# A two-layer transformer on one Trainium2 core: layer two's first query unit takes its last tile of keys as a segment of its own

## The chip, the core and the metric

The kernel runs on one core of one Trainium2 chip. The metric is the device time of one execution in microseconds, as the median of several runs. The profile is that of one further execution, taken by the hardware profiler.

The engines are TensorE (PE in the profile, PEld its weight loads), VectorE (DVE), ScalarE (ACT), GpSimd (POOL) and SyncE (SP), which issues most DMAs; POOL issues some. Each engine takes its instructions in the order written. Matmul results go to PSUM, of which the kernel uses eight banks: one for the running sum of value products, seven in one shared pool.

## The reference

Two layers, each an attention with one key and value head for 16 query heads of 28 elements, and a gated feed-forward part; x has 2048 rows of 448.

```python
def _A_ref(x, wq, wk, wv, wo):
    q = (x @ wq).reshape(B, S, H, Dh).transpose(0, 2, 1, 3)
    k = x @ wk
    v = x @ wv
    scores = einsum("bhqd,bkd->bhqk", q, k) * (Dh ** -0.5)
    o = einsum("bhqk,bkd->bhqd", softmax(scores), v)
    return o.transpose(0, 2, 1, 3).reshape(B, S, H * Dh) @ wo
def _B_ref(x, w_gate, w_up, w_down):
    return (sigmoid(x @ w_gate) * (x @ w_up)) @ w_down
for _ in range(2):
    x = x + _A_ref(_layernorm(x), A_wq, A_wk, A_wv, A_wo)
    x = x + _B_ref(_layernorm(x), B_w_gate, B_w_up, B_w_down)
```

The softmax subtracts each row's maximum over all 2048 keys.

## The kernel before, in words

**Units and steps.** A unit u is 128 queries with all 16 heads, so a layer (l = 0 or 1 in the code) has 16 units. Keys come in 16 tiles of 128, kt. The main loop (line 1081) runs 256 steps a layer, 16 for each unit. A step makes four score products (line 584, 512 columns each, four heads at a time), four exps on ScalarE into a tile P (line 587), and, one or two steps later, value products (pv, line 595: eight matmuls for a step) that add into the one bank for value sums. After a unit's last key tile ScalarE copies the sum to pvs (line 599).

**Order by hand.** PATHS gives the order inside an even and an odd step: S a score with its exp, P the value products of one waiting step, M a place for maxima, X a tick of the side chains, F a slice of filler. For layer two's first three units it is path C, "FFSXSSSPPM" in even and "SFFXFFSMSSF" in odd steps.

**Filler.** Everything on TensorE that isn't attention (query projections, gate, up and down products) comes from generators that fill.slice runs a few matmuls at a time, first in, first out. In layer two's first steps only query projections of later blocks are in it; the first feed-forward block (bulk) is added when units 0 and 1 have been normed.

**Maxima.** The row maxima are found before the scores, from rough products (mx, line 549): a group is four matmuls over up to 512 keys into four banks of the shared pool, and four reductions on VectorE (line 554). A unit has 16 groups; unit 0 of layer two has finer ones at the end, group 14 for keys 1792 to 1920 and group 15 for the last 128. When all groups of a unit are done, row_max (line 565) reduces them to a row m; a few places later fin turns m on TensorE (mt, line 575), copies it to mr (line 577), and POOL issues a DMA (line 578) that writes it as row 28 of the query tile QS, from where the score product itself subtracts it. Scores of a unit may thus start only when the row has landed. In layer two's first 48 steps a group is done at M only in the steps listed in sparse (line 1071): i * 47 // n for i below n, where n is the number of groups of units 0 to 3 still open, plus four. Else M only visits the list late, whose entries are the fins that wait.

**The seam of the layers.** When layer one's steps are over, a tail loop (line 1131) runs the last feed-forward block, and between its slices groups of maxima for layer two's units 0 to 3, as far as keys are there. For each finished tile of 128 rows a chain of stages follows: norm (db), turn (dct), keys and values (dd), turn of the keys (det), and df, which counts the tile as done (KVD). The list fine gets an entry when the last tile's output is there and another after its turn; from the first on, slices come after the stages. Group 14 of unit 0 may go only when fine holds two entries. The loop ends when all chains are empty and all groups of unit 0 are done. A further slice of filler follows (line 1151, QCH, the cost of eleven query products), then the waiting fins run (line 1062), another half slice (line 1078), and the steps of layer two begin.

**Query projection of block 1.** Its four groups of eleven products (qp) are filler at the seam. ScalarE copies each result twice, POOL subtracts (line 414) and issues the store to DRAM (qd, line 421).

**Buffers.** h has HB buffers, the scratch tag s2 three, pvs one, P twelve; at the start the first HB row tiles of x lie in h's buffers, the others in P's.

## Time and profile before

| what | value |
|---|---|
| time, median of 3 runs | 2247.47 us (2243.81 to 2251.59) |
| the profiled execution | 2247.71 us, span 2245.9 us |
| TensorE busy | 2195.5 us (98%) |
| VectorE busy | 1643.7 us (73%) |
| ScalarE busy | 1552.8 us (69%) |
| GpSimd busy | 335.9 us (15%) |
| exps (line 587) | 2048 of 690 ns in the mean |
| reductions of maxima (line 554) | 2048 of 682 ns in the mean |

The span runs from the first to the last instruction; the time holds a little more. A row of a timeline has the start and the length in us, the engine, the line, the operation, what is written from what, the shapes and how many instructions were merged (x4); in square brackets stands how long the engine had been idle before it and what ended that. Matmuls are pipelined and their ends are modelled, so starts are the safer reading. A time such as 1222.88 counts from the start of the span. The seam of the layers lies near 1220 us.

### The profile page before, as it was taken

The numbers are of one execution on the slowest core, as the hardware profiler recorded it, in microseconds if no ns is written. First come the engines' busy times: TensorE is split into PE (matmuls) and PEld (weight loads), VectorE is DVE, ScalarE is ACT, GpSimd is POOL, SyncE is SP. The second block draws the span as 40 slices with busy tenths as digits, with TensorE's granted clock in tenths as the row PEclk, the third lists the DMA queues.
The fourth block names the chain that finished last, engine by engine and source line by source line (L and its number), as shares of the span: only waits on it lengthen the run. The fifth ranks groups of instructions, "written<-read, shape, count | busy, mean of one in ns | idle before, by whom it ended". The sixth has DMA issues, their size and how long they took to land.

```text
span 2245.9 us, 41454 instructions
## 1 busy us (share of the span) xinstructions
PE 2195.5 (98%) x15915; PEld 1030.8 (46%) x15915; DVE 1643.7 (73%) x2905; ACT 1552.8 (69%) x2595; POOL 335.9 (15%) x590
## 2 busy tenths in 40 slices
PE   7998999999999999999999999999999999999999
PEld 3322344444544445454564324445454544445467
DVE  7888888777777787777796557777777777777222
ACT  5698777776667677676614997777676767777741
POOL 5113764101010100101012010000000000000010
PEclk9999999999999999999999999999999999999999
DMA  4333662323313232331441113323231313223233
GB/s 143 106 97 94 197 215 81 106 79 85 112 60 102 64 100 90 97 107 49 119 154 35 36 52 108 80 88 99 67 108 49 100 59 103 76 88 96 75 118 108
DMA packets 203622, 213.28 MB, mean 95 GB/s; under 512 B 135376, under 2 KB 164240, under 8 KB 203424
## 3 DMA queue, kind: packets, MB, share of 16 engines
q1 hardware_dynamic: 198080, 195.78, 29.2%
q0 software_dynamic: 5344, 14.87, 1.9%
q8 instruction: 124, 2.03, 0.4%
q14 instruction: 74, 0.61, 0.1%
HBM read 175.37 MB, written 23.59 MB: 89 GB/s over the span
## 4 chain that ended last, share of the span: by engine, by line
PE 86%; DVE 8%; ACT 2%; issue 1%; DMA 1%; SPq 1%; POOL 0%; DVEq 0%; ACTq 0%; POOLq 0%
PE pv L595 20%; PE s L584 19%; PE up L352 11%; PE dn L784 11%; PE gp L352 11%; PE mx L549 7%; DVE mp L554 6%; PE wo L695 3%; PE qp L352 2%; ACT P L587 1%; DMA wgu<-wgu_d 0%; DMA rq<-in_A_wq_dram 0%; DMA rc<-sums 0%; PE hot L916 0%; DVE sgu L131 0%
## 5 line engine op out<-in xcount | busy, mean ns | idle before, releaser
L587 ACT ACTIVATE P<-s,esc 128x512 f32<-128x512 f32 x2048 | 1297.8, 690 | 474.5 <-PE s L584 462.8
L554 DVE TENSOR_REDUCE mp<-mx 128x1 f32<-128x512 f32 x2048 | 1269.4, 682 | 389.2 <-PE mx L549 385.4
L584 PE MATMUL s<-QS,KK 96*128 96x512 f16 x2048 | 673.8, 381 | 21.3 <-DVE mp L554 14.8
L352 PEld LDWEIGHTS <-wgu 128*128 128x128 f16 x4928 | 467.6, 97 | 182.1 <-issue 42.9
L595 PE MATMUL pv<-P,VV 128*32 128x512 f32 x4096 | 510.7, 602 | 0.0
L352 PE MATMUL gp<-XT,wgu 128*128 128x256 f16 x2464 | 349.2, 272 | 2.4 <-DVE mp L554 1.7
L352 PE MATMUL up<-XT,wgu 128*128 128x256 f16 x2464 | 348.3, 272 | 0.7 <-DVE mp L554 0.7
L784 PE MATMUL dn<-WD,h 128*128 128x448 f16 x1344 | 301.0, 352 | 0.0
L584 PEld LDWEIGHTS <-KK 96*128 96x128 f16 x2048 | 189.7, 97 | 212.5 <-issue 114.5
L595 PEld LDWEIGHTS pv<-P,VV 128*32 128x32 f32 x4096 | 98.7, 108 | 244.6 <-issue 242.6
L549 PE MATMUL mx<-KK,QH 32*128 32x512 f16 x1792 | 185.3, 386 | 3.0 <-DVE mp L554 1.7
L784 PEld LDWEIGHTS <-h 128*128 128x128 f16 x1344 | 126.5, 97 | 129.4 <-issue 14.5
L549 PEld LDWEIGHTS <-QH 32*128 32x128 f16 x1792 | 46.0, 91 | 256.5 <-issue 252.7
L669 POOL TENSOR_TENSOR lb<-pvs,lb 128x512 f32<-128x512 f32 x32 | 41.1, 1284 | 739.1 <-DMA lb<-sums 619.8
L757 ACT ACTIVATE h<-th 128x512 f16<-128x512 f32 x112 | 70.3, 628 | 61.8 <-DVE th L754 61.5
L754 DVE SCALAR_TENSOR_TENSOR th<-th,up 128x512 f32<-128x512 f32 x112 | 76.2, 680 | 48.9 <-PE up L352 42.2
L306 POOL TENSOR_SCALAR rs<-mv 128x1 f32<-128x1 f32 (+1 forms) x50 | 11.2, 225 | 656.6 <-DVE mv L291 573.6
L352 PE MATMUL qp<-XT,WQ 128*128 128x512 f16 x352 | 108.3, 390 | 0.7 <-DVE mp L554 0.4
L746 ACT ACTIVATE th<-gp,gsc 128x512 f32<-128x512 f32 x112 | 76.8, 685 | 32.8 <-PE gp L352 32.6
L758 DVE SCALAR_TENSOR_TENSOR h<-th,h 128x512 f16<-128x512 f32 x112 | 79.9, 713 | 20.8 <-ACT h L757 20.8
L695 PE MATMUL wo<-WO,oT 128*128 128x448 f16 x384 | 89.7, 352 | 0.2 <-ACT P L587 0.2
L352 PEld LDWEIGHTS <-WQ 128*128 128x128 f16 x352 | 32.9, 99 | 54.9 <-issue 28.9
(151 smaller groups left out, 918.1 us busy)
## 6 DMA issues: line engine op xcount, KB each, us to landing
wgu<-wgu_d SPq DMA_DIRECT2D x224, 512.0 KB
QS<-qd SPq DMA_DIRECT2D x384, 32.0 KB
lb<-sums SPq DMA_DIRECT2D x128, 64.0 KB
xr<-in_A_x_dram SPq DMA_DIRECT2D x32, 224.0 KB
qd<-qst POOLq DMA_DIRECT2D x28, 256.0 KB, 2.7
wgu_d<-sgu POOLq DMA_DIRECT2D x14, 512.0 KB, 3.7
x2d<-x SPq DMA_DIRECT2D x16, 224.0 KB
xr<-x2d SPq DMA_DIRECT2D x16, 224.0 KB
```

Source lines behind the costliest of these rows:

```text
L352: nc.tensor.matmul(ps, a, b, start=n == 0, stop=n == 10)
L549: nc.tensor.matmul(ps[h][:, i * w:(i + 1) * w], qh[32 * h:32 * h + 32, g], KK[l][32 * h:32 * h + 32, 1, ka:kz], start=True, stop=True, til ...
L554: nc.vector.tensor_reduce(o, ps[h].rearrange("p (g k) -> p g k", g=n), axis=AX.X, op=OP.max)
L584: nc.tensor.matmul(s, KK[l][0:96, 0, kt * 128:(kt + 1) * 128], QS[l, u][:, g].rearrange("p h n -> p (h n)"), start=True, stop=True)
L587: nc.scalar.activation(p, s, AF.Exp, scale=esc)
L595: nc.tensor.matmul(v[32 * g:32 * g + 32], VV[l][:, kt], P[g], start=kt == 0, stop=kt == KT - 1, tile_position=(0, 32 * g))
L695: nc.tensor.matmul(p, v["oT"][:, a, h * 128:(h + 1) * 128], WO[:, c, h], start=n == 0, stop=n == 11)
L746: defer(lambda: nc.scalar.activation(th, gp.rearrange("p j n -> p (j n)"), AF.Tanh, scale=gsc))
L754: nc.vector.scalar_tensor_tensor(t, th, 1.0, up.rearrange("p j n -> p (j n)"), op0=OP.add, op1=OP.mult)
L757: nc.scalar.activation(h[:, 0], t, AF.Copy, scale=2.0 ** -17)
L758: defer(lambda: nc.vector.scalar_tensor_tensor(h[:, 1], t, 2.0 ** -17, h[:, 0], op0=OP.mult, op1=OP.subtract), 3)
L784: nc.tensor.matmul(p, hs[f // 2][:, a, o:o + 128], WD[:, f, c], start=n == 0, stop=n == 3 * FC - 1)
```

## The change

Unit 0 of layer two (halved) is split into two segments: key tiles 0 to 14, and tile 15 (CUT). The first fifteen steps use a row of maxima over 1920 keys; when they are through, a second row over all 2048 keys is written into the same place of QS, and step 15 uses it. Value sums of the two segments are separate: the first is copied to pva, multiplied by exp(old row - new row), which is spread over the partitions by way of DRAM (fd, fb), and added to the second on POOL.

The tail loop ends when fine is not empty and all groups of unit 0 but group 15 are done; stages of tile 15 that are left then run at the ticks of layer two's first steps, and df follows two ticks after det instead of five. At M of the first 48 steps the first group whose keys are there is taken; groups of units 0 and 1 are done in every step, others in the steps of sparse. The fin of unit 1 waits for one visit instead of four. A fin of the second segment waits until the scores of the first have been issued. HB goes from 10 to 8, s2 from 3 to 2 buffers, pvs from 1 to 2. Tables (STEPS, FETCH, ENDS) replace the arithmetic on step numbers.

```diff
-    TB, WB, HB = 2, 4, 10
+    TB, WB, HB = 2, 4, 8
...
-                f = wk1.tile([128, 512], F32, tag="s2", name="qf", bufs=3)
+                f = wk1.tile([128, 512], F32, tag="s2", name="qf", bufs=2)
...
+    QS, QH, PVS, PVA, ROW = {}, {}, {}, {}, {}
+    fd = [drm.tile([16, 128], F32, name=f"fd{i}") for i in range(2)]
+    fsc = cst.tile([128, 1], F32, name="fsc")
+    CUT = 15
+    scaled, SCB = set(), {}
+
+    def rescale(l, u):
+        if (l, u) in SCB and (l, u) in PVA:
+            nc.gpsimd.tensor_tensor(PVA[l, u], PVA[l, u], SCB.pop((l, u)), op=OP.mult)
+            scaled.add((l, u))
+
+    def halved(l, u):
+        return l == 1 and u == 0
+
+    def segments(l):
+        out = []
+        for u in range(U):
+            out += [(u, 0, CUT), (u, CUT, KT)] if halved(l, u) else [(u, 0, KT)]
+        return out
...
-        ends = [0, 512, 1024, 1536] + ([1792, 1920] if l and u == 0 else []) + [2048]
+        ends = [0, 512, 1024, 1536] + ([1792, 1920] if l and (u == 0 or halved(l, u)) else []) + [2048]
...
-            self.left = {u: len(groups_of(l, u)) for u in range(U)}
+            self.left = {}
+            for a in todo:
+                p = a[0], self.part(a)
+                self.left[p] = self.left.get(p, 0) + 1
...
+        def part(self, a):
+            return int(halved(self.l, a[0]) and groups_of(self.l, a[0])[a[1]][1] >= CUT * 128)
...
-            return not any(a[0] == 0 for a in self.todo)
+            return not any(a[0] == 0 and not (halved(self.l, 0) and self.part(a)) for a in self.todo)
...
-                if late[i][0] <= 0 and late[i][2] in QS:
+                if late[i][0] <= 0 and late[i][2] in QS and (not late[i][3] or ("s",) + late[i][2] in stored):
...
-            self.left[u] -= 1
-            if not self.left[u]:
-                row_max(l, u, self.mp.pop(u), todo[-1][0] + 1)
+            p = self.part((u, j))
+            self.left[u, p] -= 1
+            if not self.left[u, p]:
+                whole = p or not halved(l, u)
+                row_max(l, u, mp, todo[-1][0] + 1 if whole else kb + 1, p)
+                if whole:
+                    self.mp.pop(u)
...
-    def row_max(l, u, mp, n):
+    def row_max(l, u, mp, n, part):
...
-            stored.add(("m", l, u))
+            stored.add(("m", l, u, part))
             p = fps([16, 128], F16, "mt")
             nc.tensor.transpose(p, m16, id16)
-            r = wk1.tile([16, 128], F16, name="mr")
+            if halved(l, u) and not part:
+                r = ROW[l, u] = wk1.tile([16, 128], F16, name="mra", bufs=1)
+            else:
+                r = wk1.tile([16, 128], F16, name="mr")
             nc.vector.tensor_copy(r, p)
             (nc.gpsimd if l or u else nc.sync).dma_start(QS[l, u][28:29].rearrange("o g h n -> o (g h) n"), r)
-        late.append([4 if l and u in AHEAD else LT, fin, (l, u)])
-
-    def scores(l, u, kt, g, P):
-        assert ("m", l, u) in stored, (l, u, kt)
+            if part:
+                f = wk1.tile([16, 128], F32, tag="s2", name="fe", bufs=2)
+                nc.vector.tensor_tensor(f, r, ROW.pop((l, u)), op=OP.subtract)
+                nc.scalar.activation(f, f, AF.Exp, scale=fsc[0:16])
+                nc.sync.dma_start(fd[u % 2], f)
+                v = {}
+
+                def spread():
+                    v["b"] = wk1.tile([128, 512], F32, tag="lb", name="fb", bufs=1)
+                    for g in range(G):
+                        nc.sync.dma_start(v["b"][32 * g:32 * g + 32], fd[u % 2].rearrange("(g h) n -> g (h n)", g=G)[g:g + 1]
+                                          .to_broadcast([32, 512]))
+                    return
+                    yield
+
+                def scale():
+                    SCB[l, u] = v["b"]
+                    rescale(l, u)
+                    return
+                    yield
+                later((1, spread), (1, scale))
+        late.append([4 if l and u in AHEAD[1:] else LT, fin, (l, u), part])
+
+    def scores(l, u, kt, a, z, g, P):
+        assert ("m", l, u, int(a > 0)) in stored, (l, u, kt)
...
+        if kt == z - 1 and g == G - 1:
+            stored.add(("s", l, u))
+
+    def pv(l, u, kt, a, z, P):
+        if kt == a:
             PVS[l, u] = psv.tile([128, 512], F32, tag="v", name="pv")
         v = PVS[l, u]
         for g in range(4):
-            nc.tensor.matmul(v[32 * g:32 * g + 32], VV[l][:, kt], P[g], start=kt == 0, stop=kt == KT - 1,
+            nc.tensor.matmul(v[32 * g:32 * g + 32], VV[l][:, kt], P[g], start=kt == a, stop=kt == z - 1,
                              tile_position=(0, 32 * g))
-        if kt == KT - 1:
-            o = wk1.tile([128, 512], F32, name="pvs", bufs=1)
+        if kt == z - 1 and z < KT:
+            o = PVA[l, u] = wk1.tile([128, 512], F32, name="pva", bufs=1)
             nc.scalar.copy(o, v)
+            rescale(l, u)
+        elif kt == z - 1:
+            o = wk1.tile([128, 512], F32, name="pvs", bufs=2)
+            nc.scalar.copy(o, v)
+            if a:
+                assert (l, u) in scaled
+                nc.gpsimd.tensor_tensor(o, o, PVA.pop((l, u)), op=OP.add)
             PVS[l, u] = o
...
-                th = wk1.tile([128, 512], F32, tag="s2", name="th", bufs=3)
+                th = wk1.tile([128, 512], F32, tag="s2", name="th", bufs=2)
...
-                    later((2, db), (1, dct), (1, dd), (1, det), (5, df))
+                    later((2, db), (1, dct), (1, dd), (1, det), (2, df))
...
-        junk = wk1.tile([128, D], F32, tag="s2", name="junq", bufs=3)
+        junk = wk1.tile([128, D], F32, tag="s2", name="junq", bufs=2)
...
+        nc.vector.tensor_scalar(fsc, esc, 32768.0, None, op0=OP.mult)
...
+    STEPS, FETCH, ENDS = {}, {}, {}
+    for l in range(layers):
+        seg = segments(l)
+        STEPS[l] = [(u, kt, a, z) for u, a, z in seg for kt in range(a, z)]
+        end = {u: i for i, (u, *_) in enumerate(STEPS[l])}
+        begin = {u: min(i for i, t in enumerate(STEPS[l]) if t[0] == u) for u in range(U)}
+        FETCH[l] = {begin[u - 1] + 2: u for u in range(1, U)}
+        ENDS[l] = {i + 2: u for u, i in end.items()}
...
-            u, kt = divmod(step, KT)
+            u, kt, lo, hi = STEPS[l][step]
...
-            for o in pair[kt % 2]:
+            for o in pair[step % 2]:
                 if o == "S":
-                    scores(l, u, kt, len(P), P)
+                    scores(l, u, kt, lo, hi, len(P), P)
                 elif o == "M":
+                    a = next((a for a in mx.todo if not l or KVD[l] * 128 >= mx.need(a)), None)
                     if l and step < 3 * KT:
-                        n = step in sparse
+                        n = int(step in sparse or a[0] < 2) if a else 0
                     else:
                         n = 1 + (u == 0 and kt in MORE)
                     if not n:
                         mx.visit()
                     for _ in range(n):
-                        if not mx.step() and not final and l + 1 in mxs:
+                        if not mx.step(a if l else None) and not final and l + 1 in mxs:
                             a = mxs[l + 1].between()
                             if a and soon(a[0], mxs[l + 1].need(a)):
                                 mxs[l + 1].step(a)
-                    if kt == 2 and u + 1 < U:
-                        load_qs(l, u + 1)
+                    if step in FETCH[l]:
+                        load_qs(l, FETCH[l][step])
...
-                    if u and kt == 1:
-                        b = (u - 1) // TB
-                        if (l, b) not in BLK:
-                            BLK[l, b] = Block(l, b)
-                        later(*BLK[l, b].tile(u - 1))
+                    if step in ENDS[l]:
+                        w = ENDS[l][step]
+                        if (l, w // TB) not in BLK:
+                            BLK[l, w // TB] = Block(l, w // TB)
+                        later(*BLK[l, w // TB].tile(w))
...
-            waiting.append((l, u, kt, P))
+            waiting.append((l, u, kt, lo, hi, P))
...
-        while side or pend or (fill.gens if final else not nx.started()):
+        while (side or pend or fill.gens) if final else not (fine and nx.started()):
```

3 lines of the change are left out of this document (removed).

## The prediction

> **What bounds the kernel now.** I read the page first, then a table of windows over the run, then the engines' timelines around the layers' seam, and last the steps behind it.
>
> ```profile
> span 2245.9 us, 41454 instructions
> PE 2195.5 (98%) x15915; PEld 1030.8 (46%) x15915; DVE 1643.7 (73%) x2905; ACT 1552.8 (69%) x2595; POOL 335.9 (15%) x590
> ```
>
> ```profile
> 1200.00:1220.00 20.00, 16.61 (x143) 8.15 (x141) 14.81 (x31) 8.26 (x18) 7.94 (x10) 0.99 0.24 72
> 1220.00:1240.00 20.00, 19.10 (x105) 6.07 (x105) 8.45 (x15) 16.60 (x29) 1.75 (x3) 0.92 0.08 27
> 1225.00:1345.00 120.00, 115.62 (x718) 36.53 (x718) 67.36 (x119) 112.51 (x191) 12.94 (x25) 1.00 0.14 41
> 1500.00:1600.00 100.00, 99.81 (x739) 47.98 (x732) 78.30 (x134) 70.62 (x115) 9.01 (x20) 1.00 0.24 72
> ```
>
> The windows' columns are the stretch, its length, busy time of PE, weight loads, DVE, ACT and POOL, granted clock, DMA share and rate. TensorE is full nearly everywhere (99.81 of 100 us at 1500). Two places are not. At the seam, 1200 to 1220, it is idle for 3.39 us. From 1225 to 1345, layer two's first three units, nothing of its feed-forward work is ready; there TensorE (115.62 of 120) and ScalarE (112.51) are both nearly full. What delays that stretch delays the end, because the full stretch behind it cannot catch up. Here is the seam on TensorE:
>
> ```profile
> 1212.46 0.34 PE L335 MATMUL t<-id,hl 128*128 128x128 f16 x3 [0.24 <-DVE hl L323]
> 1212.73 0.40 PE L549 MATMUL mx<-KK,QHB 32*128 32x128 f16 x16
> 1213.07 1.47 PE L352 MATMUL qp<-XT,WQ 128*128 128x512 f16 x6
> 1214.37 0.45 PE L352 MATMUL kv<-WKV,XT 128*128 128x56 f16 x11
> 1214.66 1.46 PE L352 MATMUL qp<-XT,WQ 128*128 128x512 f16 x6
> ...
> 1216.07 0.38 PE L352 MATMUL qp<-XT,WQ 128*128 128x512 f16 x1
> 1216.69 0.41 PE L549 MATMUL mx<-KK,QHB 32*128 32x128 f16 x16 [0.24 <-ACT KK L392]
> 1220.14 0.28 PE L575 MATMUL mt<-id,m 128*16 128x128 f16 x1 [3.05 <-DVE m L570]
> 1220.35 2.74 PE L352 MATMUL qp<-XT,WQ 128*128 128x512 f16 x6
> 1222.88 1.10 PE L584 MATMUL s<-QS,KK 96*128 96x512 f16 x4
> ```
>
> Tile 15 is turned (t), group 14 of unit 0's maxima runs, then its keys (kv), then group 15 (1216.69); 3.05 us pass until the row of maxima is turned (mt), 2.74 more until the first score. The six products at 1220.35 need 2.53 us instead of 1.3 (six by 0.22, as in the row at 1214.66): after the idle time the clock is halved, as the 0.92 of that window says. So 3.05 + 0.24 + 0.24 + 1.2, or 4.7 us, is the most that the seam can give.
>
> **The seam after the change.** By the code the tail's loop ends one turn after tile 15's transposes, since group 14 may go only then (fine must hold two entries). Norm and turn thus stay ahead of the steps; keys and group 15 move behind. Left between group 14 and the scores are the 13 query products (6, 6 and 1 above), the row's turn and its DMA.
>
> ```profile
> 1213.16 2.49 DVE L554 TENSOR_REDUCE mp<-mx 128x4 f32<-128x512 f32 x4 [0.76 <-PE mx L549]
> ...
> 1219.62 0.25 DVE L569 TENSOR_REDUCE m<-mp 128x16 f32<-128x96 f32 x1
> ```
>
> ```profile
> 1217.52 0.73 POOL L421 DMA_DIRECT2D qd<-qst  x1 [1.41 <-DMA qd<-qst]
> 1218.27 1.16 POOL L414 TENSOR_TENSOR qst<-qf,qst 128x512 f16<-128x512 f32 x1
> 1219.74 0.73 POOL L421 DMA_DIRECT2D qd<-qst  x1 [0.31 <-POOL qst L414]
> 1220.97 0.53 POOL L578 DMA_DIRECT2D QS<-mr  x1 [0.49 <-DVE mr L577]
> ```
>
> The first fence is DVE's timeline, the second POOL's. Group 14 is reduced by 1215.65 (1213.16 + 2.49). From the row's own maximum (1219.62) to mt (1220.14) it took 0.52, so mt could run at 1216.2, and the scores 2.74 later, at 1218.9: 4.0 us earlier. But the row's DMA is issued by POOL, and the loop is followed by a slice of filler that ends the query projection of block 1: its fourth group (subtraction at 1218.27, store at 1219.74) is then queued on POOL ahead of the row. Both are where the third store, which waited until 1217.52 for an earlier transfer, put them; nothing in the change moves that. POOL is free at 1220.47 instead of the 1220.97 at which it issued the row before. So the first score comes **0.5 us** earlier, between 0 and 4.0.
>
> What moves behind the first score costs there: keys 0.29 us of TensorE (1214.37 to 1214.66), three small copies on ScalarE, group 15 0.4. Beside two nearly full engines I take **+0.4**, from 0 (all hidden) to 0.9.
>
> **The steps: one pair of them, then two with more maxima.** A pair of steps holds eight scores, eight exps, value products of two steps, and before one group of maxima.
>
> ```profile
> 1255.69 0.40 PE L549 MATMUL mx<-KK,QHB 32*128 32x512 f16 x4
> 1256.11 2.48 DVE L554 TENSOR_REDUCE mp<-mx 128x1 f32<-128x512 f32 x4 [2.64 <-PE mx L549]
> 1256.44 4.81 ACT L587 ACTIVATE P<-s,esc 128x512 f32<-128x512 f32 x8 [0.20 <-PE s L584]
> 1257.45 0.38 PE L584 MATMUL s<-QS,KK 96*128 96x512 f16 x1 [0.18 <-DVE mp L554]
> 1259.06 1.93 PE L595 MATMUL pv<-P,VV 128*32 128x512 f32 x16
> 1260.92 0.40 PE L549 MATMUL mx<-KK,QHB 32*128 32x512 f16 x4
> ```
>
> ```profile
> L549 PE MATMUL mx<-KK,QHB x76: 371/385/385, 1223.9 to 1319.9; 32*128 32x512 f16 x76
> ```
>
> ```profile
> 98.30:124.20 25.90, 10.74 (x32) 3.11 (x32) 1.00 0.11 39
> 1232.00:1284.40 52.40, 24.82 (x81) 7.73 (x81) 1.00 0.12 34
> ...
> 98.30:124.20 25.90, 3.15 (x32) 0.80 (x32) 1.00 0.11 39
> 1232.00:1284.40 52.40, 4.07 (x40) 1.01 (x40) 1.00 0.12 34
> ```
>
> The pair lasts 5.23 us (1255.69 to 1260.92). A group holds four of the seven banks that scores share; the score at 1257.45 waits for the second reduction. The last four rows are windows of the scores (first two) and of the maxima (last two). In layer one's early stage, 25.90 us hold 32 scores and 32 maxima matmuls, two groups a pair: 6.48 us a pair. In layer two 52.40 us hold 80 scores and 40 maxima matmuls, one group a pair: 5.24. A second group costs 1.24.
>
> The 76 matmuls are 19 groups of units 1 to 3 left at layer two's start. The old list of chosen steps has 19 + 4 = 23 entries, all even: 0, 2, 4. The new one has 24, and i*47//24 gives 0 and then odd steps: 1, 3, 5. Beside it the new rule forces a group in every step once the keys are there (step 3): group 15, then unit 1's four, steps 3 to 7. So groups run in 0, 1, 3, 4, 5, 6, 7 and then every odd step: 26 instead of 23. Three pairs (0-1, 4-5, 6-7) get a second one; two at 1.24, the first, which has no value products yet, at half: 3.1. Later, where TensorE is full, two groups fewer remain (one of unit 0 is added): -0.8, at 0.40 a group. Net **+2.3**, from 0.4 (only TensorE's 0.40 for each of the three, less 0.8) to 3.7 (three at 1.24, nothing back).
>
> From step 8 on the group stands inside the odd step instead of at the even one's end, in about 20 pairs. No row of layer two shows that order. At best it frees the wait ahead of the score at 1257.45 (0.18 a pair, -3.6). At worst the scores ahead of the value products wait for one more of the four reductions (2.48/4 = 0.6 us) in every third pair, while a query product holds a bank of its own: 0.2 a pair, +4. I take **+1**, near the middle, for want of a nearer row.
>
> **The cut at step 15.** The second row of maxima overwrites the first in the query tile, so it may go only when step 14's scores are out; the code lets it go at step 14's last place, and step 15 begins with a score. TensorE works in order, so everything behind that score waits: filler, value products, the group.
>
> ```profile
> 1250.41 0.22 PE L575 MATMUL mt<-id,m 128*16 128x128 f16 x1
> ...
> 1250.67 0.21 DVE L577 COPY mr<-mt 16x128 f16<-16x128 f16 x1 [1.03 <-PE mt L575]
> ...
> 1251.18 0.52 POOL L578 DMA_DIRECT2D QS<-mr  x1 [0.51 <-DVE mr L577]
> ...
> 1263.48 3.00 ACT L587 ACTIVATE P<-s,esc 128x512 f32<-128x512 f32 x5
> ...
> 1264.18 1.92 PE L595 MATMUL pv<-P,VV 128*32 128x512 f32 x16
> ...
> 1266.33 0.63 ACT L599 COPY pvs<-pv 128x512 f32<-128x512 f32 x1
> ```
>
> At the seam mt to score took 2.74 us; unit 1's row took nearly the same from mt to its issue, 0.77 (1250.41 to 1251.18) against 0.83. With 0.28 for mt itself TensorE stands 2.5 us, and ScalarE runs dry meanwhile. **+2.4**, from 1.2 (exps still queued cover half) to 3.0.
>
> The value products of step 14 and of step 15 now go to different sums, but there is one bank for them. In the row at 1264.18 both run as one block of sixteen; the copy at 1266.33 came when five exps ahead of it on ScalarE were through. After the change step 14's eight end at 1265.1 of that clock, the copy still waits for the exps until 1266.33 and ends at 1266.96, and step 15's eight, due at 1265.1, stand behind it: **+1.9**, from 0.6 (the copy alone) to 2.5. Rescaling and adding lie on POOL, which was idle there, and only the unit's row sums wait for them: nothing.
>
> **Clock.** 3.05 us of idling cost 1.2 us at half rate. After the change TensorE has its query products done by about 1217.5 and stands until 1222.4, and again 2.5 us at step 15; in each place some of the slow work lies beside ScalarE's. Half a microsecond each: **+1.0**, from 0 to 2.4. The Trainium skill (TensorE: Matmul & The Clock Gate, Part 1) says that the clock falls after about one idle window of 3.4 us; by it the first wait would count and the second not, and the sum would be 0.5 lower. The row at 1220.35 disagrees: 3.05 us were enough.
>
> **Edits at nothing.** Two h buffers and one scratch buffer fewer: seven h live in a block and value products of the block ahead are through before the next block's first h; the next block's gate and up products hide the exchange, and without that cover a block's first h would come late by about a copy (0.63 at 1266.33). Fetch and end tables give the same steps as before for whole units.
>
> **Sum.** -0.5 + 0.4 + 2.3 + 1.0 + 2.4 + 1.9 + 1.0 = +8.5 us; all ends together reach from -5.4 to +16.5. The profiled execution took 2247.7 us (1.8 of it outside the span) and becomes 2256.2; the median of the runs, 2247.5, lies 0.2 below: 2256.0. About 0.3% (6.7 us) is what a measurement can tell from no change.
>
> **Rivals.** *POOL is not in the way*: the scores start at 1218.9, 3.5 more is won, sum +5.0: 2252.5. For it: the store's place depends on one slice; against it: seven products remain and the slice has room for eleven. 0.15. *The steps absorb the added groups*: with the groups in odd steps a pair falls to ScalarE's 4.81, which is 0.43 less in 20 pairs, -8.6 in place of +1.0: 2246.4, not slower. It decides if the reductions always end before the fourth score behind them; the 6.48 us pairs speak against it. 0.15. *Both, and the cut half hidden by queued exps*: 3.5 and 1.2 less again, 2241.7, at the edge of faster. 0.1. *The odd steps drag*: +4 in place of +1, and the clock's upper end, 1.4 more: 2260.4. 0.1. That the change does only half of what it says, since the turn stays ahead of the steps, is in the forecast.
>
> My forecast has 0.5. The range, 2243 to 2264, takes in the first two rivals, the fourth, and the upper ends. Slower by over 0.3%, above 2254.2: three quarters of the forecast, the fourth rival and a third of the first, 0.52. Faster by as much, below 2240.7: most of the third rival, 0.09. Within: 0.39.
>
> **What would show it.** After: the row's DMA on POOL right behind a store (near 1220.5); first score 1222.4; groups in steps 3 to 7 with pairs over 6 us; a gap of 2.5 us ahead of step 15's first score, put down to the QS DMA; one near 2 us ahead of pv at step 16, put down to ScalarE. I am wrong if the first score comes near 1219, or if 48 steps last no longer than before.

## The result, and the profile after

| | before | after |
|---|---|---|
| time, median of 3 runs | 2247.47 us (2243.81 to 2251.59) | 2268.36 us (2267.41 to 2269.84) |
| profiled execution | 2247.71 us, span 2245.9 | 2268.36 us, span 2266.6 |

After by before is 1.0102, with a 95% interval of 1.0088 to 1.0115 (the two medians alone give 1.0093): slower by about 21 us, where 8.5 were predicted and 2264 was the upper end. The page of the kernel after, in the lines that were shown of before (span, busy time of the engines):

```profile
span 2266.6 us, 41491 instructions
PE 2206.3 (97%) x15916; PEld 1029.9 (45%) x15916; DVE 1643.1 (72%) x2910; ACT 1557.4 (69%) x2597; POOL 341.2 (15%) x593
```

TensorE has one matmul more, and is busy 10.8 us longer: matmuls that run at half clock last longer (the score at 1227.94 below takes 0.63 us, the one at 1222.40, which starts at full clock, 0.39), and matmuls that start further apart overlap less. The other 10 us are idle time. To see where both lie, both traces are cut at the same pieces of work: the first score of layer two's step 0, then of steps 2, 8, 14, 16, 18, 48, and 64 to the last. (The time of layer one differs by some us between any two profiles, even of kernels that are equal up to there, so everything is counted from layer two's first score.) Kernel before, a table of windows (stretch, its length, busy time and count of PE, weight loads, DVE, ACT, POOL, then granted clock, DMA share, rate):

```profile
1222.88:1226.79 3.91, 3.50 (x17) 1.31 (x15) 2.45 (x4) 3.41 (x6) 0.00 (x0) 0.98 0.00 0
1226.79:1242.27 15.48, 14.96 (x96) 4.63 (x95) 7.48 (x13) 15.13 (x27) 0.75 (x1) 1.00 0.05 18
1242.27:1258.10 15.83, 15.41 (x97) 4.79 (x96) 8.96 (x18) 15.05 (x26) 1.25 (x2) 1.00 0.05 18
1258.10:1263.12 5.02, 4.84 (x33) 1.51 (x32) 2.28 (x4) 4.60 (x9) 0.00 (x0) 1.00 0.00 0
1263.12:1268.45 5.33, 5.09 (x32) 1.50 (x31) 2.69 (x6) 5.33 (x11) 0.00 (x0) 1.00 0.01 2
1268.45:1350.46 82.01, 79.20 (x491) 25.22 (x490) 45.99 (x82) 75.70 (x129) 12.12 (x24) 1.00 0.20 56
...
1412.05:2155.81 743.76, 743.18 (x5465) 358.42 (x5462) 529.66 (x903) 538.60 (x871) 54.73 (x119) 1.00 0.27 83
```

The same steps of the kernel after:

```profile
1222.40:1230.31 7.91, 6.36 (x31) 1.83 (x32) 3.74 (x7) 5.20 (x11) 0.00 (x0) 0.52 0.00 0
1230.31:1252.07 21.76, 20.38 (x115) 5.52 (x114) 13.11 (x24) 15.53 (x27) 0.75 (x1) 0.86 0.04 13
1252.07:1269.12 17.05, 16.06 (x97) 4.62 (x96) 8.71 (x17) 15.03 (x26) 1.27 (x2) 1.00 0.05 17
1269.12:1276.71 7.59, 5.26 (x34) 1.51 (x33) 2.82 (x7) 5.16 (x10) 0.52 (x1) 1.00 0.08 22
1276.71:1283.97 7.26, 5.87 (x34) 1.46 (x33) 2.91 (x6) 6.07 (x12) 2.54 (x2) 1.00 0.06 15
1283.97:1371.20 87.23, 82.34 (x493) 24.81 (x491) 46.39 (x83) 76.11 (x128) 12.24 (x24) 1.00 0.19 52
...
1432.79:2175.59 742.80, 742.30 (x5457) 358.12 (x5454) 523.50 (x895) 539.69 (x871) 55.36 (x119) 1.00 0.28 83
```

Row by row, the second column of one minus that of the other gives the account of the change. Steps 0 and 1 lose 4.0 us (7.91 against 3.91, at a clock of 0.52). Steps 2 to 7 lose 6.3, the six behind them 1.2, the pair with the cut 2.6, the pair behind it 1.9, steps 18 to 47 lose 5.2, and the long full stretch gives 1.0 back. With the first score 0.5 earlier the sum is 19.7 of the 20.7 us by which the span grew.

TensorE's timeline of the kernel after at the seam (start, duration, engine, line, operation, tiles, shapes, count; in brackets the idle time before it and what ended it):

```profile
1216.03 0.22 PE L604 MATMUL mt<-id,m 128*16 128x128 f16 x1 [0.17 <-DVE m L599]
1216.18 1.47 PE L352 MATMUL qp<-XT,WQ 128*128 128x512 f16 x6
1222.40 0.39 PE L637 MATMUL s<-QS,KK 96*128 96x512 f16 x1 [4.75 <-DMA QS<-mra]
1222.63 0.64 PE L352 MATMUL kv<-WKV,XT 128*128 128x56 f16 x11
1223.08 1.46 PE L637 MATMUL s<-QS,KK 96*128 96x512 f16 x3
1224.48 1.15 PE L574 MATMUL mx<-KK,QHB 32*128 32x512 f16 x4
...
1227.75 0.29 PE L388 MATMUL kvt<-id,ktl 128*128 128x128 f16 x1 [1.55 <-DVE ktl L381]
...
1227.94 0.63 PE L637 MATMUL s<-QS,KK 96*128 96x512 f16 x1
```

POOL's queue at the same place:

```profile
1219.58 0.73 POOL L421 DMA_DIRECT2D qd<-qst  x1 [0.31 <-POOL qst L414]
1220.31 0.53 POOL L610 DMA_DIRECT2D QS<-mra  x1
```

The row of maxima was turned at 1216.03, as predicted, and its DMA went out at 1220.31, directly behind the fourth store of the query projection. TensorE stood for 4.75 us, and the first score came at 1222.40, where the prediction had it. The moved keys then show a second wait that the prediction did not have: their turn (1227.75) stands 1.55 us for the copies of the keys, which are behind an exp on ScalarE and behind a group's reductions on VectorE. And from 1222.7 the clock record shows half rate for 10.2 us, then once more for 3.4 us from 1243.2; in the kernel before, seam and steps together had one stretch of 3.4 us. The cut, in the same timeline:

```profile
1272.04 0.22 PE L604 MATMUL mt<-id,m 128*16 128x128 f16 x1
1274.39 0.39 PE L637 MATMUL s<-QS,KK 96*128 96x512 f16 x1 [2.14 <-DMA QS<-mr]
...
1278.03 1.07 PE L650 MATMUL pv<-P,VV 128*32 128x512 f32 x8
1280.23 1.06 PE L650 MATMUL pv<-P,VV 128*32 128x512 f32 x8 [1.13 <-ACT pva L654]
```

From the row's turn to the score 2.35 us pass, and the second eight value products wait for the copy of the first sum (pva): both waits are those predicted, at the places predicted, and both are shorter (2.14 us for 2.5, and 1.13 for near 2).

### The profile page after: what moved, and what is told of

Same layout as the page of the kernel before. It is cut to its first block, busy times and chain, and to the rows that moved or that the text cites. A ratio compares the mean times of both kernels' runs of the same rounds, so it can differ in the third digit from the quotient of the medians.

```text
span 2266.6 us, 41491 instructions
## 1 busy us (share of the span) xinstructions
PE 2206.3 (97%) x15916; PEld 1029.9 (45%) x15916; DVE 1643.1 (72%) x2910; ACT 1557.4 (69%) x2597; POOL 341.2 (15%) x593
## 4 chain that ended last, share of the span: by engine, by line
PE 84%; DVE 8%; ACT 3%; DMA 2%; issue 1%; SPq 1%; POOL 1%; DVEq 0%; ACTq 0%; POOLq 0%
PE pv L650 20%; PE s L637 19%; PE dn L846 11%; PE up L352 11%; PE gp L352 11%; PE mx L574 7%; DVE mp L579 6%; PE wo L757 3%; ACT P L640 2%; PE qp L352 2%; DMA rc<-sums 1%; POOL qst L414 0%; DMA rq<-in_A_wq_dram 0%; DMA wgu<-wgu_d 0%; PE hot L978 0%
## 5 line engine op out<-in xcount | busy, mean ns | idle before, releaser
L637 PE MATMUL s<-QS,KK 96*128 96x512 f16 x2048 | 683.1, 383 | 31.3 <-DVE mp L579 10.4
```

What stands on the lines that cost most here:

```text
L637: nc.tensor.matmul(s, KK[l][0:96, 0, kt * 128:(kt + 1) * 128], QS[l, u][:, g].rearrange("p h n -> p (h n)"), start=True, stop=True)
```

## The experiments

What had to be told apart after this result: **A**, the chosen steps that turned from even to odd places cost the time of steps 8 to 48; **B**, it is the lower clock, brought by the waits; **C**, it is the crowding of forced groups in steps 3 to 7; and, for the seam, whether POOL's queue holds the first score. Each run is compared with the kernel before on the same chip (medians of 2246.0, 2246.4 and 2245.6 us in the three groups of runs).

**1. The old kernel with odd places.** One entry more in the list, nothing else.

```diff
-            n = sum(a[0] < 4 for a in mx.todo) + 4
+            n = sum(a[0] < 4 for a in mx.todo) + 5
```

> The kernel before, with one more in the count of the sparse list (24 entries), so that the groups of maxima in layer two's first 48 steps fall into odd steps, as they do after the change; nothing else. Theory A (the place inside the odd step costs 0.2 to 0.3 us a pair): about 6 us slower than before, 2253 to 2254, spread evenly over steps 2 to 48. Theory B (the place is harmless; what steps 8 to 48 lost after the change comes from its other parts): within 1 us of before.

Measured: 2259.1 us (2253.1 to 2262.0), ratio 1.0057 (1.0045 to 1.0069). So 13 us, or more than half of the loss, come to the old kernel without any of the change's parts. Its window of steps 18 to 47, and a pair of it on TensorE's timeline:

```profile
1264.96:1352.59 87.63, 82.80 (x491) 24.72 (x490) 46.24 (x83) 76.17 (x128) 11.74 (x24) 1.00 0.18 50
```

```profile
1262.74 0.78 PE L549 MATMUL mx<-KK,QHB 32*128 32x512 f16 x4
1264.21 0.59 PE L584 MATMUL s<-QS,KK 96*128 96x512 f16 x2 [0.69 <-ACT P L587]
```

87.63 us against 82.01, at full clock: A holds there, at 5.6 us in 15 pairs. Inside the odd step the group comes when two scores still have their exps to come and a query product holds a bank; its four matmuls, each as long as before (371 to 385 ns), spread over 0.78 us instead of 0.40, and the score behind them then waits 0.69 us for an exp to free a bank. From the first score to step 8 the odd places cost 2.3 us, to step 48 10.6, and to the end 13.4; the last 2.8 lie behind step 48, in the full stretch, and why is open. (The profiled execution, 2253.14 us, is the fastest of the six: its first score came at 1214.45, 8.4 us earlier than before, since layer one took less time in it. The last section comes back to that.)

**2. The new kernel with even places.**

```diff
-            n = sum(a[0] < 4 for a in mx.todo) + 4
+            n = sum(a[0] < 4 for a in mx.todo) + 3
```

> The changed kernel with one less in that count (23 entries), so that from step 8 on the groups stand at the ends of even steps again; the forced groups of steps 3 to 7, the cut and the seam stay. Theory A: steps 8 to 48 win back about 6 us, time 2262. Theory B: 2268 as after the change.

Measured: 2264.59 us (2261.07 to 2266.84), ratio 1.0082 (1.0069 to 1.0095). The loss of steps 8 to 13 is gone (15.97 us, 5.40 + 10.57, against 15.83), but steps 18 to 47 are no shorter (87.71). Two places hold that time; here both on TensorE's timeline, then the first on VectorE's:

```profile
1296.69 0.54 PE L757 MATMUL wo<-WO,oT 128*128 128x448 f16 x2
1298.65 0.93 PE L757 MATMUL wo<-WO,oT 128*128 128x448 f16 x4 [1.42 <-DVE oT L738]
...
1344.10 0.93 PE L757 MATMUL wo<-WO,oT 128*128 128x448 f16 x4 [1.86 <-DVE oT L738]
```

```profile
1295.52 2.48 DVE L579 TENSOR_REDUCE mp<-mx 128x1 f32<-128x512 f32 x4 [1.30 <-PE mx L574]
1297.92 0.68 DVE L738 TENSOR_TENSOR oT<-lb,oT 128x512 f16<-128x512 f32 x1
```

In steps 24 and 25 unit 0's output product waits for its normalization, which came to VectorE behind four reductions: 2.2 us. In steps 40 to 43, where unit 1's output product (1344.10) waits in the same way, there are 3.7 more, with half clock from 1345.6 for 3.4 us. So moving the list back took one loss away and brought two others; theory A's 2262 did not come.

**3. The first row's DMA from SyncE.**

```diff
-            (nc.gpsimd if l or u else nc.sync).dma_start(QS[l, u][28:29]...
+            (nc.gpsimd if (l or u) and not (halved(l, u) and not part) else nc.sync).dma_start(QS[l, u][28:29]...
```

> The changed kernel with the first row of maxima written by a DMA from SyncE instead of POOL, so that it does not queue behind the stores of the query projection. If POOL's queue alone held the first score, the score comes 3.5 us earlier (near 1218.9 of the span) and the time falls by about that, to 2265. If the 10.2 us at half clock behind the 4.75 us wait are what made the first pairs of steps long, the wait of some 1.3 us leaves the clock whole, the first pair falls from 7.9 to about 5 us and the time to 2261 or less.

Measured: 2261.63 us (2256.40 to 2264.93), ratio 1.0068 (1.0054 to 1.0082). TensorE's first score:

```profile
1216.62 0.39 PE L637 MATMUL s<-QS,KK 96*128 96x512 f16 x1 [0.72 <-DMA QS<-mra]
```

It waits 0.72 us instead of 4.75 and comes 112.95 us behind the first score of layer one's last step, against 116.69: 3.7 us earlier, the 3.5 that the first rival had put on POOL's queue. But the clock did not stay up, so the median came near the second of the expected times, 2261, without the reason given for it: the first pair of steps still took 7.13 us. The clock fell at 1220.6, for 6.8 us, with no wait of TensorE longer than 1.31 us around it, and at the cut, for 10.2 us, where steps 16 and 17 took 10.15 instead of 7.26:

```profile
1269.56:1279.71 10.15, 9.36 (x33) 1.81 (x32) 2.53 (x5) 6.30 (x11) 2.53 (x2) 0.55 0.02 6
```

**4 and 5. Keeping TensorE busy.** Unused products of the identity into the bank of value sums, 22 ahead of step 0; in the second kernel six more in each of steps 0 and 1.

```diff
+        if l:
+            hot2 = psv.tile([128, 512], F32, tag="v", name="hot2")
+            for _ in range(22):
+                nc.tensor.matmul(hot2, id16, id16.rearrange("p (o j) -> p o j", o=1).to_broadcast([128, 4, 128]),
+                                 start=True, stop=True)
```

> The changed kernel with 22 matmuls of the identity added ahead of the first step, which fill TensorE's 4.75 us wait and compute nothing that is used; the first score stays at 1222.4. Clock theory: no half rate, the first pair of steps 4.5 to 5 us instead of 7.9 and the next three a little shorter, time 2264. Rival (the keys' turn that waits on ScalarE, and the crowded maxima, made them long): at most 1 us less, 2267 to 2268.

> The changed kernel with 22 unused identity matmuls ahead of its first step and 6 each in steps 0 and 1, so that TensorE stays active until value products begin. Clock theory: no half rate before step 10; steps 0 to 10 then lose 5.5 to 6 us against before instead of 10.4 (the line through the other runs: 5.7 us and 0.4 for each us of half rate); time about 2263. Rival: the half rate is a mark of the waits and not their cause; steps 0 to 10 stay within 1 us of the run with 22 alone, 7.1.

Measured: 2264.46 us (2263.53 to 2267.33), ratio 1.0086 (1.0071 to 1.0101), with half clock for 3.4 us at 1224.3 and at 1268.7; and 2266.31 us (2265.52 to 2267.75), ratio 1.0093 (1.0079 to 1.0107), with none in layer two until the last microseconds. The second kernel's steps 0 to 3, 4 to 7 and 18 to 47:

```profile
1222.27:1229.65 7.38, 6.88 (x43) 2.54 (x43) 3.49 (x7) 4.97 (x10) 0.00 (x0) 1.00 0.00 0
1229.65:1235.09 5.44, 5.26 (x44) 1.55 (x43) 2.42 (x5) 4.76 (x9) 0.00 (x0) 1.00 0.01 3
1235.09:1249.03 13.94, 12.68 (x72) 3.48 (x71) 10.94 (x20) 10.50 (x19) 0.75 (x1) 1.00 0.06 19
...
1280.92:1368.15 87.23, 82.34 (x492) 24.81 (x491) 46.37 (x83) 76.02 (x128) 12.21 (x24) 1.00 0.19 52
```

Steps 4 to 7 of the kernels before and after:

```profile
1232.02:1242.27 10.25, 9.89 (x64) 3.01 (x63) 5.45 (x9) 9.90 (x18) 0.75 (x1) 1.00 0.08 27
...
1236.63:1252.07 15.44, 14.18 (x72) 3.79 (x71) 10.94 (x20) 10.69 (x19) 0.75 (x1) 0.89 0.06 19
```

At full clock steps 4 to 7 take 13.94 us (after 15.44) and steps 0 to 3 take 12.82 (after 14.23), the twelve added products included. So B is worth some 3 us: 1.5 in steps 4 to 7 and 1.4 ahead of them (1.8 by the first of the two kernels, whose steps 0 to 3 take 12.39). The rest stays, above all the 87.23 of steps 18 to 47: B is not their cause. The time of the first kernel is the 2264 that the clock theory gave, but not by its way: the first pair took 6.68 us with 22 products, not 4.5 to 5, and with the second kernel's full clock steps 0 to 9 lost 7.5 us, not 5.5 to 6. That is within 1 us of the 7.1 of the first, as the rival said. The twelve products' own cost was not measured, so it stays open whether the last 3.4 us of half rate cost nothing or the products took back what the clock gave.

**6. Even places, and unit 1's groups not forced.**

```diff
-                        n = int(step in sparse or a[0] < 2) if a else 0
+                        n = int(step in sparse or a[0] < 1) if a else 0
```

(with the list as in experiment 2)

> The changed kernel with the groups at even steps (23 entries) and without the forcing of unit 1's groups: only unit 0's last group is forced, unit 1's four go in steps of the list. Theory C (two groups a pair crowd the shared banks in steps 3 to 8): steps 2 to 8 win back 4 to 5 us against the kernel with even steps alone, time about 2260. Theory D (half clock and the keys' turn make these steps long): no more than 1 us, 2264.

Measured: 2260.62 us (2258.06 to 2261.79), ratio 1.0065 (1.0045 to 1.0085). Steps 4 to 7 and 18 to 47 of this kernel:

```profile
1235.60:1246.26 10.66, 10.24 (x64) 3.09 (x63) 7.03 (x13) 9.79 (x18) 0.75 (x1) 1.00 0.08 26
...
1280.81:1362.78 81.97, 79.31 (x492) 25.48 (x491) 46.01 (x82) 75.86 (x130) 12.19 (x24) 1.00 0.21 56
```

Steps 4 to 7 of experiment 2:

```profile
1231.70:1245.70 14.00, 12.74 (x72) 3.47 (x71) 11.05 (x20) 10.55 (x19) 0.75 (x1) 1.00 0.06 20
```

Both rows have full clock, so C is 14.00 - 10.66, or 3.3 us; the prediction had 2.5 for these two pairs (two groups at 1.24). And with the even list and the units' order of before, steps 18 to 47 take 81.97 us, as they did before (82.01). The 15.7 us that this kernel still loses are all in steps 0 to 17, where the clock was down for 13.7, 3.4 and 3.4 us and TensorE stood 1.88 us for unit 1's row at 1257.83. That the median is the expected 2260 is partly luck: steps 2 to 9 won back 1.9 us (24.66 against 26.58) and not 4 to 5, and the 5.7 of steps 18 to 47 were not expected.

**7. One row only.** Unit 0 keeps the early start and its scores run with the maximum over the first 1920 keys; group 15, the second row, the second sum and the rescaling are left out.

```diff
-            out += [(u, 0, CUT), (u, CUT, KT)] if halved(l, u) else [(u, 0, KT)]
+            out += [(u, 0, KT)]
-            self.todo = todo
+            self.todo = todo = [a for a in todo if not self.part(a)]
-            n = sum(a[0] < 4 for a in mx.todo) + 4
+            n = sum(a[0] < 4 for a in mx.todo) + 5
```

> The changed kernel without the cut: unit 0's sixteen steps all use the first row of maxima, over 1920 keys, and group 15, the second row, the second sum and the rescaling are left out (a row's subtracted value then is not its maximum over all keys); the list keeps its 24 odd entries. Theory: the 2.1 us wait at step 15 and the wait for the one bank of value sums at step 16 disappear, 4.5 us less, and group 15's place 0.4 to 1 less: 2263. Rival (TensorE makes the waits good in the full stretch): 2267 to 2268.

Measured: 2268.18 us (2264.66 to 2270.16), ratio 1.0099 (1.0080 to 1.0117). Its steps 8 and 9, and 14 and 15:

```profile
1247.64:1255.52 7.88, 7.75 (x33) 1.86 (x32) 2.38 (x5) 5.12 (x10) 0.00 (x0) 0.66 0.00 1
...
1267.11:1272.39 5.28, 5.15 (x32) 1.42 (x31) 2.27 (x5) 4.66 (x8) 0.00 (x0) 1.00 0.00 0
```

The turn of unit 1's row, on TensorE:

```profile
1245.83 0.22 PE L604 MATMUL mt<-id,m 128*16 128x128 f16 x1 [2.06 <-DVE m L599]
```

The cut is gone: 5.28 us where after has 7.59, and 5.99 for the next pair where after has 7.26, 3.6 less in all. The kernel is not faster. Steps 0 to 9 take 38.76 us where after has 35.13: with group 15 gone, unit 1's last group comes earlier and its row is turned at the very next place for maxima, so TensorE stands 2.06 us for it. The clock was at half rate for 20.5 us, 13.7 from 1215.5 and 6.8 from 1246.2, right behind that wait; steps 8 and 9 take 2.4 us longer than in the kernel after. Another 2.5 us are lost behind step 48. I had expected 2263; the number is the rival's, but its reason, that TensorE makes the waits good in the full stretch, does not show: the cut's 3.6 us are won, and lost elsewhere.

**8. The turn of the keys two ticks later.**

```diff
-                    later((2, db), (1, dct), (1, dd), (1, det), (2, df))
+                    later((2, db), (1, dct), (1, dd), (3, det), (2, df))
```

> The changed kernel with tile 15's key turn two ticks later, in step 3 instead of step 1, so that it does not wait for the copies that stand behind exps on ScalarE. If that 1.5 us wait counts by itself and keeps the clock at half: the first pair of steps 2 to 3 us shorter, 2265 to 2266. If not: 2268, the wait only moving.

Measured: 2266.21 us (2264.56 to 2268.32), ratio 1.0092 (1.0075 to 1.0110). The turn of the keys:

```profile
1229.73 0.22 PE L388 MATMUL kvt<-id,ktl 128*128 128x128 f16 x1
```

The 1.55 us wait ahead of it is gone. The median is near the 2265 to 2266 expected for a wait that counts by itself, but steps 0 and 1 take 7.5 us instead of 7.9, not the 2 to 3 less that would make it so, and the clock was down for 13.7 us at the seam (after 10.2 and 3.4) and 10.2 at the cut. Steps 0 to 9, with the same groups of maxima, take 35.17 us, after 35.13: with as much half rate, taking the wait away does not shorten them. What the wait costs at full clock cannot be read from it.

**9 and 10. No query product beside the steps.** The projections of blocks 2 and 3 come into the filler at step 48; once with the old, even list (first), once with the odd one of experiment 1.

```diff
-        if l:
-            for b in range(2, NB):
-                fill.add(qgen(l, b), G * QCH)
...
+            if l and step == 3 * KT:
+                for b in range(2, NB):
+                    fill.add(qgen(l, b), G * QCH)
```

> The kernel before, with the query projections of blocks 2 and 3 put into the filler at step 48 of layer two instead of ahead of step 0, so that no query product holds a shared bank in the first 48 steps. Reference for the next run; the 88 products (19 us) move into the full stretch, the pairs of steps 8 to 46 should fall to about 4.96 us, so some 10 to 14 us slower than before.

> The same with the groups of maxima in odd steps (24 entries). Bank theory (the odd place costs because a query product holds one of the seven banks while scores, four maxima and scores pass in a row): without query products the odd place costs nothing or wins, steps 8 to 46 as long as in the run with even steps or up to 0.3 us a pair shorter. Order theory (the place itself costs, whoever holds the banks): 0.3 to 0.4 us a pair longer, 8 us in all, as with the query products.

Measured: 2253.71 us (2252.77 to 2257.25), ratio 1.0039 (1.0026 to 1.0053), and 2262.03 us (2259.35 to 2264.01), ratio 1.0073 (1.0059 to 1.0086). Steps 18 to 47 with the even list:

```profile
1261.33:1335.03 73.70, 70.82 (x442) 20.92 (x442) 43.26 (x78) 71.21 (x124) 9.15 (x20) 1.00 0.17 45
```

And with the odd list:

```profile
1268.28:1343.32 75.04, 72.27 (x443) 19.48 (x442) 43.81 (x79) 71.76 (x123) 9.14 (x20) 1.00 0.17 44
```

With the query products gone, the odd list costs 1.3 us in these 15 pairs, 1.0 of it in the two pairs with an output product, where with them it costs 5.6. The kernel after says the same within one run: of its 15 pairs the three without a query product (26 to 29, 42 and 43) lose -0.07, 0.10 and -0.07 us against before, each with a group in its odd step, and the other twelve lose 5.3 together. So it is not the place of the group alone that costs, but the place together with a query projection. That the projection costs by the bank that it keeps is argued from the waits, not shown: these two runs also take its work off TensorE and its copies off ScalarE, and ScalarE is then the fuller of the two (busy 71.21 of 73.70 us, TensorE 70.82). The odd list is still 8.3 us slower in the medians, though hardly in the pairs. From the first score on the two profiled executions differ by 6.5: 2.4 in steps 0 to 3, where this kernel had half clock for 13.7 us and the other for 10.2, 1.3 in steps 18 to 47, and 2.8 behind step 48, as in experiment 1 and as unexplained.

**11 and 12. All of it undone.** One row only, its DMA from SyncE, nothing forced but unit 0, the even list that then follows, the keys' turn two ticks later (edits of 7, 3, 6, 8; the list keeps its + 4). The second kernel has also unit 1's row one visit later and 3, 6 and 6 unused products. Both leave out what experiment 7 leaves out.

```diff
-        late.append([4 if l and u in AHEAD[1:] else LT, fin, (l, u), part])
+        late.append([4 if l and u in AHEAD[1:] else 2 if l and u == 1 else LT, fin, (l, u), part])
```

> Everything that the theory names, undone together, on top of the changed kernel: one row of maxima over 1920 keys for unit 0 (no cut, no second row), the row's DMA from SyncE, groups at even steps, no forcing of unit 1, the keys' turn two ticks later. If the named causes are all there is: first score 4 us earlier than before, first pair some 1 us longer, the rest as before: 2243 to 2245 against 2246. If the rest of the change costs something unnamed (buffers, tables, later row sums): 2248 or more.

> The run that undid everything named, with unit 1's row turned one step later (its turn had waited 2.06 us for the reductions just ahead of it and brought half rate with it) and 3, 6 and 6 unused identity matmuls ahead of and in steps 0 and 1. If both stalls go: first score 4 us earlier than before and no more than 2 us lost in the first 48 steps, so 2 us below before, at the edge of what 5 rounds tell; if half rate finds another wait: as before.

Measured: 2245.72 us (12 runs, 2242.43 to 2250.16), ratio 1.0000 (0.9990 to 1.0010), and 2244.76 us (11 runs, 2240.37 to 2247.43), ratio 0.9993 (0.9984 to 1.0002). The first lost 3.7 us in steps 12 to 15, where TensorE waited 2.06 us for unit 1's row and had half clock behind it. The second's steps 0 and 1, and 18 to 47:

```profile
1218.37:1224.61 6.24, 6.00 (x36) 2.45 (x37) 2.58 (x5) 3.98 (x8) 1.63 (x2) 1.00 0.53 148
...
1267.09:1349.05 81.96, 79.31 (x492) 25.40 (x491) 45.99 (x82) 75.59 (x129) 12.16 (x24) 1.00 0.20 56
```

In layer two it falls to half clock only in the last microseconds, its first score is 4.3 us earlier than before (112.64 us behind layer one's last step, before 116.99), and steps 0 to 47 lose 3.1 of that. The 1.2 us left are below what these runs can tell from no change. So the named causes together carry the loss but for 3.1 us in steps 0 to 47, and no version here is shown to be faster than the kernel before.

## Why the prediction was wrong in size

**Right.** The first score and POOL's store ahead of the row (-0.5 and -0.5; experiment 3 gives the 3.7 us that the queue holds). The steps in which groups run, and the crowding of steps 4 to 7 (2.5 and 3.3; the 3.1 counted the first pair too). The cut (2.4 predicted) and the one bank of value sums (1.9): against before these pairs lose 2.6 and 1.9, but part of that is the odd list's, and against experiment 7, which has no cut, they lose 2.3 and 1.3. The groups that are missing later (-0.8 and -1.0). The buffers and tables, which stay in experiment 12, at nothing: from step 64 to the last score it takes 746.3 us, as before. These give about 5 of the 20 us. All upper ends of the prediction together, +16.5, fall short of the result.

**The step that failed most: "From step 8 on ... I take +1".** It measured 6.4 us in the kernel after (1.2 in steps 8 to 13, 5.2 in 18 to 47; 7.3 with the odd list's 0.9 in steps 14 to 17) and 8.2 in experiment 1: beyond the bound of +4 too. The mechanism of that bound fits what came, a score waiting for one more reduction or exp while a query product is under way, but it was counted "in every third pair". The timelines show query products in twelve of the fifteen pairs from step 18 on, mostly three to five where a sum takes eleven, so a sum is open, and keeps its bank, most of the time; 0.35 us a pair came, where 0.2 was the worst case. Experiments 9 and 10 show that the query products are the condition (not that it is their bank), experiment 6 that the even place, with unit 1 not forced, takes the loss back. The fourth rival, "the odd steps drag", was this case, with 0.1.

**The clock: +1.0, "half a microsecond each".** It is worth 3 us (experiments 4 and 5: 1.5 in steps 4 to 7, 1.4 to 1.8 ahead of them). The prediction counted the half rate as one stretch behind each wait. After the first wait it lasted 10.2 us, in steps 0 to 3, where TensorE stood for the keys and waited for banks (busy 6.36 of the first pair's 7.91 us), and 3.4 us came again at 1243.2. At the cut nothing came in after; in experiments 3 and 8 the same wait brought 10.2 us. By the rule cited from the Trainium skill (TensorE: Matmul & The Clock Gate, Part 1) only an idle window of 3.4 us lowers the clock. The length of the half-rate stretches agrees with such a window, 3.4, 6.8, 10.2 and 13.7 us. The idle time does not: 1.31 us and less around 1220.6 in experiment 3, 2.06 in experiments 7 and 11. The same part of the page tells, under "A second HAM failure mode", of small gaps between groups of matmuls that make the clock go up and down; that is nearer to what these steps show.

**The moved keys: +0.4.** Steps 0 to 3 lose 5.1 us (14.23 against 9.14). At full clock, with the added products, experiment 5 still loses 3.7 there (12.82 - 9.14). The prediction priced the work, 0.29 and 0.4 us of TensorE and small copies, and had no term for the wait of 1.55 us in front of the turn, where the copies stand behind an exp on ScalarE and four reductions on VectorE. But experiment 8 took that wait away and steps 0 to 9 were no shorter, so the wait isn't shown to be the price. I did not measure how the 3.7 divide between it, the groups in steps 1 and 3 and the added products; this part stays open.

**"Only the unit's row sums wait for them: nothing"** holds as far as the runs show. In experiment 2 unit 0's normalization came behind four reductions and cost 2.2 us, but unit 1's, which has no cut, waited in the same way; in experiment 6, with the same rescaling, the pair of steps 24 and 25 took 7.10 us (before 6.94). It depended on where a group stood.

Summed, the account of the loss is: odd places from step 8 on 7.3; steps 0 to 7, crowding of 4 to 7 at full clock 3.7 (13.94 against 10.25), clock about 3, and the rest, keys and first groups, about 3.6; cut and bank 3.6; first score and later groups -1.5. That is 19.7.

Left open: why the odd lists of experiments 1 and 10 lose 2.8 us behind step 48, and that of experiment 7 2.5 against after; whether the query projection costs by its bank or by its work; and what exactly lowers the clock.

## What to carry to other kernels

A list of places that is computed from a count can flip as a whole when the count changes by one; after such a change, compare which steps were chosen before pricing anything else. When a pool of banks is shared by short tiles and long accumulations, ask how much of the time an accumulation is open, and put groups that need several banks at once where the pool is least used. When work is moved into a full stretch, look at the queues that its small copies join as well as at its work; and before you call the wait that you find there the price, take it away alone, as experiment 8 does. An edit that is meant to remove one wait can bring another: in experiments 6, 7 and 11 unit 1's row, turned after one visit instead of four, held TensorE for about 2 us, and only the timeline shows it.

## What the hardware showed unexpectedly

TensorE's clock fell to half rate in stretches of 3.4 us or two, three or four times that: up to 13.7 us, in four of the kernels here. All stretches of one execution lie on one grid with a step of 3.413 us. In the kernel after they begin at 28.05, 48.53, 92.90, 130.45, 1222.71 and 1243.19 us, all whole multiples of the step apart. Where the grid lies differs from execution to execution. So the same wait can fall inside one step of the grid or across two. At the cut TensorE stands the same 2.1 to 2.2 us in the kernel after, where the wait crosses a grid line at 1273.91, 1.66 us after it begins, and in experiment 3, where 1.91 of its 2.17 us lie inside one step. The step that holds most of the wait, in the kernel after and then in experiment 3:

```profile
1270.50:1273.91 3.41, 1.76 (x17) 0.35 (x9) 0.52 (x3) 1.92 (x4) 0.52 (x1) 1.00 0.00 0
...
1264.97:1268.38 3.41, 1.50 (x9) 0.52 (x10) 0.39 (x2) 1.45 (x3) 0.52 (x1) 1.00 0.07 21
```

The clock stayed up behind the first and fell at the end of the second. TensorE was busy 1.76 and, in experiment 5, 1.62 of 3.41 us where it stayed, and 1.27 to 1.59 where it fell (experiments 2, 3, 4 and 8). That is no limit for other places: the step ahead of 1243.19 in the kernel after was busy 2.71 us, and the clock fell. What else counts is not shown.

Kernels with the same code at the seam had 10.2 us (experiment 2) or 13.7 (experiment 6). With the odd list and the forced groups, steps 0 to 9 lose more with more half rate: 8.6 us with 6.8 (experiment 3) and 10.4 with 13.7 (the kernel after, and experiment 8), and 7.1 with 3.4 where 22 products were added (experiment 4), or about 0.3 us for each microsecond; waits that come with the half rate are in these figures. Layer one varies along with it: the kernel after and those with its code up to the seam reached the first score at 1222.3 to 1222.4 us when the opening of layer one had 17.1 us of half rate (after, experiment 5), and at 1216.5 to 1217.0 when it had 3.4 (experiments 2, 7 and 8); the kernel before, with 17.1, reached it at 1222.9, and experiment 1, with 3.4, at 1214.5. So one profile does not price a wait here: the same steps 16 and 17 took 7.26 us in one kernel and 10.15 in another that differs only at the seam, at a clock of 1.00 and 0.55.
